# A time budget for VectorE's side work, row scalings on ScalarE, and split fills in neighbouring places, in an attention-with-gradient kernel

## The chip, the cores and the metric

The kernel runs on one core of a Trainium2 chip. The metric is the device time of one execution in microseconds (us). Every kernel was run several times, in alternation with the kernel before on the same chip.

The engines go by short names in the profile. **TensorE** runs matmuls and is called PE in the profile; **VectorE** is DVE, **ScalarE** is ACT, **GpSimd** is POOL, and SP is the engine whose queue issues most DMAs. In this kernel the results of TensorE go to tiles in a memory called **PSUM**, in *banks*; other tiles lie in **SBUF**. A *releaser* is what ended a wait.

## The reference

The reference is a small transformer block with two branches, and the gradient of all its inputs. It was cut here to what matters:

```python
B, T, D, K = (2, 4000, 144, 5)
xa = _layernorm(x)
q, k, v = split(xa @ w_qkv)
p = softmax(q @ k.T * D ** -0.5)
glob = (p @ v) @ w_att_out
h = gelu(xa @ w_mlp_in);  u, g = halves(h);  g = _layernorm(g)
gc = sum(gp[:, i:i + T, :] * dw_csgu[i] for i in range(K))     # 5-tap convolution over time
loc = (u * gc) @ w_mlp_out
m = concat([glob, loc]);  m = m + 5-tap convolution of m
out = x + m @ w_merge
# asked for: out, and the gradients of x and of all seven weights for a given grad_out
```

There are two batches of 4000 rows, which the kernel treats one after the other. Rows come in 32 blocks of 128 (`NBK`), that is 16 *row pairs* (`NPR`).

## The kernel before

For each batch there is one long stage, called *attention* below, in which two kinds of work are interleaved:

- the **global part**: scores, softmax and their gradients, in 129 *units*. A unit is a quarter of one row block; in it TensorE makes four score tiles (`pS` for this unit, `pD` for the one before), ScalarE takes the exponential of `pS`, VectorE makes `Sm = pD * P`. After its unit, TensorE multiplies into `y` and into `X` (the *fills*), whose results are added to `acc` by VectorE (even fills) or by ScalarE and GpSimd (odd fills);
- the **local part** (MLP, layer norm, convolutions), cut into small steps. Each unit has two *places* in which local steps may be issued. For each row pair a Python generator yields before each step: `'V'` for a step without matmuls, `'P'` for one with, and what it must come after.

All of this decides only the order of issue. In the traces an engine works off its list in order (below, ScalarE stands idle for 2.24 us before one instruction while copies stand behind it). The parts that matter:

```python
class Steps:
    def _ready(self, t):
        at, w, _ = t
        if self.now < at: return False
        if w is None: return True
        kind, lag, after = w
        return all(key in self.done and self.now >= self.done[key] + d for key, d in after)
    ...
    def place(self, tensor=True):
        again = True
        while again:                       # every V step that is ready, at once
            again = False
            for t in list(self.tasks):
                if (t[1] is None or t[1][0] == 'V') and self._ready(t):
                    self._step(t)
                    again = True
        if tensor:                         # then one P step
            due = [...]
            if due: self._step(min(due, key=lambda t: t[0]))
        self.now += 1

    def pair(p):                           # local steps of one row pair, cut
        ...
        yield 'V', 2, aft(("dh", 3))       # after the dh of pair p - 3 was issued
        dh = wk.tile([128, 2, 2 * D], BF, tag="dh", bufs=3, name="dh")
        ...
        nc.vector.tensor_tensor(ug[:], h_[:, :, 0:D], gc[:], op=ALU.mult)
        nc.vector.tensor_tensor(du[:], dug[:], gc[:], op=ALU.mult)
        nc.vector.tensor_tensor(dh[:, :, 0:D], du[:], gp[:, :, 0:D], op=ALU.mult)
        ...
        yield 'P', 1, aft(("dg", 1), ("dh", 3), ("wg", 4))
        dgC.put(p, dgc)                    # 4 transposes into PSUM, ScalarE copies out, 16 rows to DRAM
        Q.mark("dg", p)
        yield 'V', 2
        dgC.fill(p)                        # loads the 80 rows of taps that conv needs
        yield 'P', 4, ((("dg", min(p + 1, NPR - 1)), 6),) + aft(("dh", 1))
        pc = dgC.conv(p, True)             # TensorE; waits for the 80-row load
        ...
        nc.vector.tensor_tensor(dh[:, :, D:2 * D], dg[:], gp[:, :, D:2 * D], op=ALU.mult)
        nc.sync.dma_start(S.dh_d[:, 2 * p:2 * p + 2, :], dh[:])
        Q.mark("dh", p)

    def wgrad(p):                          # weight gradient of the convolution
        yield 'V', 2, ((("dg", p), 2),)
        d8 = wk.tile([128, 256], BF, tag="d8", bufs=2, name="d8")
        dgC.taps.spread(d8[0:80, :], p * 256, 256)      # another load from the same DRAM rows
        for m in range(5): ...

    for p in range(NPR):
        Q.add(14 * p, pair(p))
        Q.add(14 * p + 20, wgrad(p))

        def row_end(i):                    # after the last unit of row block i
            nc.vector.reduce_sum(ld[:], ld8[:], axis=AX.X)
            nc.vector.reciprocal(rl[:], ld[:, 0:1])
            nc.vector.tensor_scalar(nd[:], ld[:, 1:2], rl[:], -1.0, op0=ALU.mult, op1=ALU.mult)
            nc.vector.tensor_scalar(Qs[:, pb, :], S.Q_t[:, i, :], rl[:], None, op0=ALU.mult)
            nc.vector.tensor_scalar(br[:], S.B_t[:, i, :], rl[:], None, op0=ALU.mult)
            nc.vector.scalar_tensor_tensor(Bt[:, pb, :], Qs[:, pb, :], nd[:], br[:], op0=ALU.mult, op1=ALU.add)
```

`pm`, `pc`, `ph`, `pj` (local part) and `X` (fills) share three PSUM banks. A fill of a row pair sums over both row blocks of the pair; fills 0 and 1 are split, so that the first block's half can be done early and its bank is held open until the second.

## Time and profile before

| | before |
|---|---|
| median of the first three runs | 1318.11 us (1311.19 to 1318.71) |
| attention, first and second batch | about 66 to 561 us and 696 to 1188 us of the span |
| TensorE busy in attention, by stretch of 33 us | 90 to 99% (the prediction below says 93 to 98%; two stretches with a dip of the clock have 90%) |
| VectorE busy in attention, by stretch of 33 us | 19.9 to 30.4 us |

The first part of the page of the kernel before gives the busy time of each engine, its share of the span and the instructions:

```profile
PE 1222.5 (93%) x15116; PEld 957.1 (73%) x15116; DVE 986.3 (75%) x3421; ACT 806.0 (61%) x2370; POOL 580.4 (44%) x1033
```

TensorE's 93% overstates its work, since records of pipelined matmuls overlap (a 144-column matmul has a record of 226 ns and the next one starts after 62 to 63). I therefore count *gaps* from the starts of the matmuls in the trace. The 144-column matmuls start every 62 to 63 ns when nothing holds them up. Whatever a start comes later than that is a gap, put down to the matmul that came late. It is an estimate, and it comes to 107 us for both batches, of which 6.6 us are what matmuls lost at half clock.

The list of waits of TensorE from 66 to 1196 us, kernel before (what waited, for what: us in total, times, longest us), sees only that part of each gap in which no older matmul was still in its record. It is good for naming the releaser:

```profile
PE X L1925 <- DVE acc L1939: 14.8, 16, 2.8
PE pc L1574 <- DMA gnC<-gnC_d: 9.1, 8, 2.1
PE pD L1854 <- DVE Sm L1868: 7.4, 26, 0.7
PE pm L1545 <- ACT sq L1686: 2.8, 4, 0.8
PE pm L1545 <- ACT dgf L1760: 1.8, 2, 0.9
```

### The profile page before, as it was taken

The numbers are of one execution on the slowest core, as the hardware profiler recorded it, in microseconds if no ns is written. First come the engines' busy times: TensorE is split into PE (matmuls) and PEld (weight loads), VectorE is DVE, ScalarE is ACT, GpSimd is POOL, SyncE is SP. The second block draws the span as 40 slices with busy tenths as digits, with TensorE's granted clock in tenths as the row PEclk, the third lists the DMA queues.
The fourth block names the chain that finished last, engine by engine and source line by source line (L and its number), as shares of the span: only waits on it lengthen the run. The fifth ranks groups of instructions, "written<-read, shape, count | busy, mean of one in ns | idle before, by whom it ended". The sixth has DMA issues, their size and how long they took to land. (4 is left out here: it accounts for less than half of the span.)

```text
span 1318.5 us, 39927 instructions
## 1 busy us (share of the span) xinstructions
PE 1222.5 (93%) x15116; PEld 957.1 (73%) x15116; DVE 986.3 (75%) x3421; ACT 806.0 (61%) x2370; POOL 580.4 (44%) x1033
## 2 busy tenths in 40 slices
PE   4899999999999999999989999999999999999986
PEld 2657776777777777798976677677777777779884
DVE  4666777887989888847735688788798888884664
ACT  2666666667667666546646666666766766654542
POOL 6312445444545454247611244545444544425640
PEclk9999999999999999999999999999999999999999
DMA  6369888887899889987775989888999988998851
GB/s 182 97 126 152 149 153 147 147 149 150 154 164 155 157 141 170 157 190 206 200 218 104 157 145 168 146 146 146 149 152 159 164 151 146 165 159 191 240 151 32
DMA packets 634223, 205.51 MB, mean 156 GB/s; under 512 B 577183, under 2 KB 631556, under 8 KB 633988
## 3 DMA queue, kind: packets, MB, share of 16 engines
q1 hardware_dynamic: 627472, 197.54, 79.3%
q10 hardware_dynamic: 6548, 5.33, 1.8%
q8 instruction: 120, 1.97, 0.6%
q14 instruction: 83, 0.68, 0.2%
HBM read 46.22 MB, written 21.79 MB: 52 GB/s over the span
## 5 line engine op out<-in xcount | busy, mean ns | idle before, releaser
L1868 DVE SCALAR_TENSOR_TENSOR Sm<-pD,Pm 128x500 bf16<-128x500 f32 x512 | 325.6, 673 | 104.0 <-PE pD L1858 71.4
L1866 ACT ACTIVATE Pm<-pS 128x500 bf16<-128x500 f32 x512 | 295.4, 584 | 99.6 <-PE pS L1858 96.8
L1925 PE MATMUL X<-Qs,Sm 128*128 128x144 bf16 x2048 | 286.5, 226 | 15.3 <-DVE acc L1939 14.8
L1937 POOL TENSOR_TENSOR acc<-xs,acc 128x432 f32<-128x432 f32 x150 | 172.3, 1148 | 268.3 <-ACT xs L1936 267.9
L1926 PE MATMUL X<-Bt,Pm 128*128 128x144 bf16 x2048 | 286.4, 226 | 0.8 <-DVE Bt L1890 0.8
L1926 PEld LDWEIGHTS <-Pm 128*128 128x128 bf16 x2048 | 200.6, 98 | 19.4 <-issue 18.4
L1925 PEld LDWEIGHTS <-Sm 128*128 128x128 bf16 x2048 | 200.5, 98 | 2.2 <-issue 1.0
L1903 PEld LDWEIGHTS <-ST 128*128 128x128 bf16 x2048 | 137.8, 98 | 28.2 <-issue 1.1
L1903 PEld LDWEIGHTS <-PT 128*128 128x128 bf16 x2048 | 137.4, 98 | 28.3 <-issue 0.5
L1936 ACT COPY xs<-X 128x432 f32<-128x432 f32 x150 | 77.7, 518 | 127.4 <-PE X L1926 113.9
L1939 DVE TENSOR_TENSOR acc<-X,acc 128x432 f32<-128x432 f32 x180 | 104.0, 578 | 65.6 <-PE X L1926 65.2
L1854 PE MATMUL pD<-rb,QBr 16*128 16x500 bf16 x448 | 100.8, 379 | 7.3 <-DVE Sm L1868 6.6
L1866 ACT ACTIVATION_READ_ACCUMULATOR Pm<-pS 128x1 f32 x512 | 103.3, 202 | 0.0
L1854 PE MATMUL pS<-rb,QBr 16*128 16x500 bf16 x448 | 92.4, 382 | 2.5 <-ACT Pm L1866 2.4
L1858 PEld LDWEIGHTS <-BTm 128*128 128x128 bf16 x512 | 50.0, 98 | 59.3 <-issue 1.5
L1785 DVE SCALAR_TENSOR_TENSOR jg<-gnC,dgC 128x256 bf16<-128x256 bf16 x160 | 92.0, 575 | 1.3
L1858 PEld LDWEIGHTS <-QTm 128*128 128x128 bf16 x512 | 29.1, 97 | 75.8 <-issue 75.8
L1913 POOL TENSOR_TENSOR B_t<-zd,yd 128x144 bf16<-128x144 f32 x64 | 34.3, 537 | 111.5 <-ACT zd L1912 111.5
L1892 POOL TENSOR_SCALAR nr<-nd,rl 128x1 f32<-128x1 f32 x64 | 20.5, 320 | 136.9 <-DVE nd L1886 136.7
L1858 PE MATMUL pS<-rb,QTm 128*128 128x500 bf16 x256 | 77.3, 384 | 0.0
L1858 PE MATMUL pS<-ra,QTm 128*128 128x500 bf16 x256 | 76.9, 382 | 0.0
L1858 PE MATMUL pD<-rb,BTm 128*128 128x500 bf16 x256 | 75.7, 377 | 0.0
(626 smaller groups left out, 2949.6 us busy)
## 6 DMA issues: line engine op xcount, KB each, us to landing
gs<-in_grad_out_dram SPq DMA_DIRECT2D x24, 720.0 KB
dh_d<-dh SPq DMA_DIRECT2D x32, 144.0 KB
dhr<-dh_d SPq DMA_DIRECT2D x16, 288.0 KB
gs<-in_grad_out_dram SPq DMA_DIRECT2D x8, 540.0 KB
xg<-in_x_dram SPq DMA_DIRECT2D x21, 144.0 KB
dug_d<-dug SPq DMA_DIRECT2D x16, 144.0 KB
dug<-dug_d SPq DMA_DIRECT2D x32, 72.0 KB
ug_d<-ug SPq DMA_DIRECT2D x32, 72.0 KB
```

The costliest lines, as they stand in the source:

```text
L1785: nc.vector.scalar_tensor_tensor(jg[:], a_[:, m:m + 256], 1.0, d_[:, 2:258], op0=ALU.mult, op1=ALU.mult, accum_out=dws[:, p, m:m + 1])
L1854: nc.tensor.matmul(o_[h][:, 0:SC], jt[i // 4][2][rr, i % 4, :], S.XR[c2][rr, 0:SC], start=True, stop=False)
L1858: nc.tensor.matmul(o_[h][:, 0:SC], jt[i // 4][w][:, i % 4, :], S.xaT[:, c0:c0 + SC], start=False, stop=True)
L1866: nc.scalar.activation(P[:, pb, c1:c1 + SC], o_[h][:, 0:SC], ACT.Exp, accum_out=ld8[:, 0, n_:n_ + 1])
L1868: nc.vector.scalar_tensor_tensor(Sm[:, pb, c1:c1 + SC], o_[h][:, 0:SC], 1.0, P[:, pb, c1:c1 + SC], op0=ALU.mult, op1=ALU.mult, accum_out=l ...
L1903: nc.tensor.matmul(y[:, w, :], src[:, jj, :], S.xaa[:, j, :], start=(j == 0), stop=(j == NBK - 1))
L1913: nc.gpsimd.tensor_tensor(S.Zn[:, i, :], zd[:], yd[:], op=ALU.add)
L1925: nc.tensor.matmul(X[:, jj, :], Sm[:, i % NP, j * 128:(j + 1) * 128], Qs[:, i % 4, :], start=(kk == 0 and jj == 0), stop=False, skip_group ...
L1926: nc.tensor.matmul(X[:, jj, :], P[:, i % NP, j * 128:(j + 1) * 128], Bt[:, i % 4, :], start=False, stop=(kk == 1), skip_group_check=True)
L1936: nc.scalar.copy(xs[:, 0:nj, :], X[:, 0:nj, :])
L1937: nc.gpsimd.tensor_tensor(a_, xs[:, 0:nj, :], a_, op=ALU.add)
L1939: nc.vector.tensor_tensor(a_, X[:, 0:nj, :], a_, op=ALU.add)
```

## The change

The intent: VectorE is busy 75% of the time and yet late, since its local steps come in lumps. So (1) a budget lets only so much VectorE time be issued per place; with it come a sorting of the tasks by the time they were set for, and a slightly closer start of the row pairs; (2) two row scalings move to ScalarE, which has time; (3) the two halves of a split fill move into neighbouring places, so that two of the three PSUM banks are held for a shorter time.

```diff
 class Steps:
+    def __init__(self, rate, most):
+        self.left, self.rate, self.most = most, rate, most
+    def use(self, cost):
+        self.left -= cost
     def _ready(self, t):
-        return all(key in self.done and self.now >= self.done[key] + d for key, d in after)
+        return all(key in self.done and self.now >= self.done[key] + d for key, d in w[2]) and (w[3] == 0 or w[0] != 'V' or self.left >= w[3] / 2)
     def _step(self, t):
+        if t[1]:
+            self.left -= t[1][3]
     def place(self, tensor=True):
+        self.left = min(self.left + self.rate, self.most)
-            for t in list(self.tasks):
+            for t in sorted(self.tasks, key=lambda t: t[0]):
 ...
-        yield 'V', 2, aft(("dh", 3))
+        yield 'V', 2, aft(("dh", 3)), 1.1          # each V step now names its cost in us
 ...                                               # (one step is split in two)
-        Q.add(14 * p, pair(p))
-        Q.add(14 * p + 20, wgrad(p))
+        Q.add(27 * p // 2, pair(p))
+        Q.add(27 * p // 2 + 20, wgrad(p))
 ...
-            nc.vector.tensor_scalar(Qs[:, pb, :], S.Q_t[:, i, :], rl[:], None, op0=ALU.mult)
+            nc.scalar.activation(Qs[:, pb, :], S.Q_t[:, i, :], ACT.Copy, scale=rl[:])
-            nc.vector.tensor_scalar(br[:], S.B_t[:, i, :], rl[:], None, op0=ALU.mult)
+            nc.scalar.activation(br[:], S.B_t[:, i, :], ACT.Copy, scale=rl[:])
+            Q.use(1)
 ...
-        fills = {(1, 0): ..., (7, 1): ((0, (0,)), (1, (0,)))}
+        fills = {(0, 1): ((0, (0,)), (1, (0,))), (1, 0): ...}      # the rest as before
-        Q = Steps()
+        Q = Steps(1.15, 1.4)
 ...                                               # the adds of the fills call Q.use(.6)
+                if i == NBK:                      # after the last row block
+                    Q.rate = Q.most = 1.8
```

More of the change, by code (lines that the diff above doesn't have):

```diff
@@ L1599 @@
 class Steps:
-    def __init__(self):
+    def __init__(self, rate, most):
         self.now, self.done, self.tasks = 0, {}, []
+        self.left, self.rate, self.most = most, rate, most
     def add(self, at, gen):
@@ L1618, in _ready @@
             return True
-        kind, lag, after = w
-        return all(key in self.done and self.now >= self.done[key] + d for key, d in after)
+        return all(key in self.done and self.now >= self.done[key] + d for key, d in w[2]) and (w[3] == 0 or w[0] != 'V' or self.left >= w[3] / 2)
     def _step(self, t):
+        if t[1]:
+            self.left -= t[1][3]
         try:
@@ L1627, in _step @@
             return
-        w = (w + ((),))[:3] if len(w) < 3 else w
+        w = tuple(w) + ((), 0)[len(w) - 2:]
         t[0], t[1] = self.now + w[1], w
     def place(self, tensor=True):
+        self.left = min(self.left + self.rate, self.most)
         again = True
@@ L1692, in pair @@
         nc.gpsimd.tensor_scalar(t3[:], sq[:], 6 * K0 * K1, 2 * K0, op0=ALU.mult, op1=ALU.add)
-        yield 'V', 2
+        yield 'V', 2, (), .5
         nc.vector.tensor_tensor(a_[:], a_[:], hs[:], op=ALU.mult)
@@ L1697, in pair @@
         nc.scalar.activation(a_[:], a_[:], ACT.Tanh)
-        yield 'V', 2, aft(("ug", 4))
+        yield 'V', 2, aft(("ug", 4)), .8
         h_ = wk.tile([128, 2, 2 * D], BF, tag="h_t", bufs=4, name="h_t")
@@ L1702, in pair @@
         Q.mark("h", p)
-        yield 'V', 1
+        yield 'V', 1, (), .95
         mv = sm.tile([128, 2, 2], F32, tag="mvg", name="mv")
@@ L1716, in pair @@
         nc.gpsimd.tensor_tensor(oq[:], oq[:], h_[:], op=ALU.mult)
-        yield 'V', 2, aft(("dh", 6))
+        yield 'V', 2, aft(("dh", 6)), 1.2
         nm = sm.tile([128, 2], F32, tag="nmg", name="nm")
@@ L1738, in pair @@
         nc.scalar.copy(gc[:], pc[:])
+        yield 'V', 0, (), .45
         dgc = wk.tile([128, 2, D], BF, tag="dgc", bufs=2, name="dgc")
         nc.vector.tensor_tensor(dgc[:], dug[:], h_[:, :, 0:D], op=ALU.mult)
-        yield 'V', 2, aft(("dh", 3))
+        yield 'V', 2, aft(("dh", 3)), 1.1
         dh = wk.tile([128, 2, 2 * D], BF, tag="dh", bufs=3, name="dh")
@@ L1760, in pair @@
             nc.scalar.activation(dg[:, q, :], pc[:, q, :], ACT.Copy, scale=rs[:, q:q + 1], accum_out=s12[:, 0, q:q + 1])
-        yield 'V', 2
+        yield 'V', 2, (), 1.1
         jk = jg[:, 0:D]
@@ L1770, in pair @@
             nc.gpsimd.tensor_scalar(cc[:, q, :], gn[:, q, :], n12[:, 1, q:q + 1], n12[:, 0, q:q + 1], op0=ALU.mult, op1=ALU.add)
-        yield 'V', 2
+        yield 'V', 2, (), .75
         nc.vector.tensor_tensor(dg[:], dg[:], cc[:], op=ALU.add)
@@ L1783, in wgrad @@
         for m in range(5):
-            yield 'V', 1
+            yield 'V', 1, (), .6
             nc.vector.scalar_tensor_tensor(jg[:], a_[:, m:m + 256], 1.0, d_[:, 2:258], op0=ALU.mult, op1=ALU.mult, accum_out=dws[:, p, m:m + 1])
-        yield 'V', 1
+        yield 'V', 1, (), .6
         nc.vector.scalar_tensor_tensor(jg[0:80, :], gnC.kept8.pop(p)[0:80, :], 1.0, d8[0:80, :], op0=ALU.mult, op1=ALU.mult, accum_out=dw8[0:80, p:p + 1])
@@ L1933, in xfill @@
                 (nc.scalar.copy if f % 2 else nc.vector.tensor_copy)(a_, X[:, 0:nj, :])
+                Q.use(0 if f % 2 else .6)
             elif f % 2 == 1:
@@ L1938, in xfill @@
             else:
+                Q.use(.6)
                 nc.vector.tensor_tensor(a_, X[:, 0:nj, :], a_, op=ALU.add)
-        fills = {(1, 0): ((0, (1,)), (1, (1,))), (1, 1): ((2, (0, 1)),), (2, 1): ((3, (0, 1)),), (3, 0): ((4, (0, 1)),), (3, 1): ((5, (0, 1)),),
-                 (4, 1): ((6, (0, 1)),), (5, 0): ((7, (0, 1)),), (5, 1): ((8, (0, 1)),), (6, 0): ((9, (0, 1)),), (6, 1): ((10, (0, 1)),), (7, 1): ((0, (0,)), (1, (0,)))}
-        Q = Steps()
+        fills = {(0, 1): ((0, (0,)), (1, (0,))), (1, 0): ((0, (1,)), (1, (1,))), (1, 1): ((2, (0, 1)),), (2, 1): ((3, (0, 1)),), (3, 0): ((4, (0, 1)),), (3, 1): ((5, (0, 1)),),
+                 (4, 1): ((6, (0, 1)),), (5, 0): ((7, (0, 1)),), (5, 1): ((8, (0, 1)),), (6, 0): ((9, (0, 1)),), (6, 1): ((10, (0, 1)),)}
+        Q = Steps(1.15, 1.4)
         local_steps(k, W, b, S, es, ps_f, Q)
@@ L1962, in phase_attn @@
                         for f, rows in fills.get((half * 4 + c2, place), ()):
-                            q = pr + 1 if rows == (0,) else pr
-                            if 0 <= q < NBK // 2:
-                                xfill(q, f, rows)
+                            if 0 <= pr < NBK // 2:
+                                xfill(pr, f, rows)
                         Q.place()
```

## The prediction

> **What bounds it now.** Each of the two batches spends about 495 us (66-561 and 696-1188 us of the span) in the attention stage; the change touches only that. There the windows view shows TensorE busy 93-98%, but busy times overlap. The timeline shows 144-column matmuls starting every 62-63 ns[...]. Counting starts that way (the four 16-row matmuls of a unit run together in about 0.32 us), I estimate 436 us of real work and 51-54 us of gaps per batch. TensorE is the bound, at about 89%; only the gaps, about 105 of 1318 us, can be won.
>
> By the instruction that came late, both batches: pD (waits for VectorE to finish Sm) 28 us; X (waits for a PSUM bank that VectorE's acc add frees) 19; pS 28, of which about 26 is a fixed 0.1 us per unit; the convolution pc (waits for its 80-row DMA) 10; transposes pm 6. So about 50 us hang on a late VectorE, though it is busy only 24-30 of 33 us per window: it is late in lumps. From issue order and measured durations, VectorE's work between Sm pairs averages 3.30 us, standard deviation 1.02; 36 of 127 intervals exceed the 3.9 us pace, up to 5.8.
>
> **What the change does.**
> 1. The budget evens VectorE's work. Same count in the changed order: standard deviation 0.74, maximum 4.8, 17 over, excess 23 -> 7 us per batch. Here is the gain.
> 2. Qs and br go to ScalarE: VectorE loses 254 + 288 ns for each of 64 rows, 35 of its 986 us. ScalarE gains two one-pointer ACTIVATEs per row: [...]the trace has 0.38 for the like zd and yd. About +50 us on ScalarE (806 -> 855), not the bound. But Bt stays next in VectorE's order after nd, so VectorE now waits about 0.5 us for ScalarE: less busy, Bt hardly earlier. ScalarE waits for rl. Worth nothing or slightly negative.
> 3. Split fills keep two of three PSUM banks open for two places instead of four; 12 matmuls now stand before the second row's Bt is needed, covering the longer row end. A few us fewer X and pm waits.
>
> Matmuls, DMA and the other stages stay; put-to-convolution distance stays three units, so pc's wait stays.
>
> **Time.** Estimate: 60% of pD and X waits (28 us), 3 of pm, minus about 6 of new ScalarE-VectorE waits: -25 us. **Predicted 1293 us, 80% range 1278-1309.** Faster by over 2%: 0.44; within 2%: 0.53; slower: 0.03.
>
> **What would show it.** Attention about 12 us shorter per batch, the rest unchanged. TensorE waits pD<-Sm and X<-acc less than half. VectorE busy about 950, with new idle before Bt, released by ScalarE's br, 0.3-0.6 us x 64. ScalarE about 855, idle before Qs released by VectorE's rl. The pc wait on DMA still about 10 us.
>
> **What would make it wrong.** ScalarE, held behind Qs, delays exps, so pS and then Sm wait. DMA engines, 79-100% busy here, may fall behind a faster TensorE, so flips or 80-row loads arrive late. Or gaps merely move to another releaser. On the other side, fewer gaps could also remove the three clock dips in attention (3.4-6.8 us at half clock), and the gain exceeds 30 us.

28 us of pD and X waits and 3 of pm, less 6 for new waits, are the 25 us that lead from 1318 to 1293. The +50 us on ScalarE, which are not in the sum, follow from 0.38 us in the trace for each of 128 instructions.

## More of the kernel before

The fills wait for a bank that VectorE frees, the score tiles for VectorE's `Sm`, the forward convolution for the load of its taps. The backward convolution's load (`dgC<-dgC_d`) does not appear.

The timeline of the SP queue, kernel before, shows why (start us, us, engine, line, operation, out<-in). The load of the taps, L1527, is issued ahead of the spread, L1524, and ahead of two transposing DMAs that occupy the queue for 2 to 3 us each:

```profile
370.93 0.40 SPq L1520 DMA_DIRECT2D dgC_d<-dgC0s  x1
371.37 0.43 SPq L1663 DMA_DIRECT2D Rz<-R_d  x1
373.30 0.31 SPq L1527 DMA_DIRECT2D dgC<-dgC_d  x1
373.66 0.75 SPq L1524 DMA_DIRECT2D d<-dgC_d  x1
374.52 2.81 SPq L1876 DMA_TRANSPOSE ST<-Sm  x1
377.42 2.38 SPq L1876 DMA_TRANSPOSE PT<-Pm  x1
```

Two stretches from the windows view, kernel before (stretch, length, busy us of each engine with its count, then granted clock, DMA share, GB/s), for comparison later:

```profile
66.00:312.00 246.00, 233.59 (x2693) 172.23 (x2693) 184.67 (x620) 159.82 (x478) 97.73 (x161) 0.98 0.84 147
529.00:560.00 31.00, 29.50 (x358) 22.02 (x355) 27.06 (x96) 17.33 (x56) 8.82 (x18) 1.00 0.95 165
```

## The result, and the profile after

The changed kernel was slower: 1331.85 us (median of four runs, 1330.61 to 1333.88) against 1316.66 us (four runs, 1311.19 to 1318.71), a ratio of 1.0123 with a 95% interval of 1.0089 to 1.0158. Ratios here and below are the mean time of one kernel's fast runs over that of the kernel before in the same rounds, so not quite the ratio of the medians that are quoted.

The first part of the page, kernel after:

```profile
PE 1226.7 (92%) x15116; PEld 959.4 (72%) x15116; DVE 962.1 (72%) x3293; ACT 843.2 (63%) x2498; POOL 561.5 (42%) x1033
```

VectorE lost 24 us of busy time (35 predicted) and ScalarE gained 37 us (about 50 predicted). The waits of TensorE from 66 to 1196 us, kernel after:

```profile
PE pc L1574 <- DMA dgC<-dgC_d: 16.6, 11, 2.8
PE X L1933 <- DVE acc L1949: 15.4, 12, 4.4
PE pm L1545 <- ACT dgC L1549: 6.3, 2, 3.2
PE pD L1861 <- DVE Sm L1875: 4.0, 18, 0.5
PE pc L1574 <- DMA gnC<-gnC_d: 1.6, 3, 0.7
```

Three lines are new or changed. The backward convolution now waits 16.6 us for its load; the longest wait for a bank grew from 2.8 to 4.4 us; the transposes `pm` wait twice for 3.2 us. Three lines of the waits of ScalarE and VectorE in the same stretch, kernel after, have no counterpart before:

```profile
ACT Qs L1894 <- DVE rl L1891: 71.0, 59, 4.1
...
DVE Bt L1898 <- ACT br L1896: 33.9, 63, 0.5
...
DVE dh L1754 <- DMA dh_d<-dh: 6.0, 2, 3.7
```

The windows view, kernel after, for the same two stretches:

```profile
66.00:312.00 246.00, 235.70 (x2757) 173.73 (x2756) 188.78 (x608) 175.01 (x529) 99.14 (x171) 0.99 0.88 153
529.00:560.00 31.00, 26.26 (x301) 19.28 (x299) 21.45 (x76) 16.10 (x51) 8.45 (x17) 0.94 0.91 157
```

In the first stretch TensorE did 2757 matmuls where it had done 2693. In the second it did 301 where it had done 358. So the changed kernel is *ahead* for half of the stage and then loses it. Units 8 to 56 of the first batch took 181.6 us (before 188.9); units 120 to 128 took 36.2 us (before 30.6), and in the second batch 35.4 us (30.6).

TensorE's gaps from the trace, by the instruction that was late, both batches. *Cold* is what matmuls lost by running at half clock; *all* contains it and some smaller ones:

| us | pD | pS | X | pc | pm | cold | all |
|---|---|---|---|---|---|---|---|
| before | 28.6 | 28.4 | 20.5 | 13.4 | 5.8 | 6.6 | 107 |
| after | 23.0 | 26.4 | 24.0 | 22.9 | 6.9 | 12.8 | 119 |

The largest gaps fall at the same units in both batches, so they belong to the order of issue. Three chains explain them.

**The dh store (unit 122).** The chain that ended last, kernel after (start us, us, what):

```profile
536.32 0.31 DVE dh L1780
536.62 0.03 DVE ug L1752
536.65 3.97 DMA dh_d<-dh
...
540.94 1.28 DVE Sm L1875 x4
542.22 0.53 DVE acc L1949
542.75 0.04 issue
542.79 0.28 PE X L1933
```

The last write of an old pair's `dh` (L1780) and the first write of a new pair's `dh` (L1754, after L1752 and L1753) now come together. With three buffers the new write must wait until the store of the old one, issued a moment before, has landed. VectorE stands for 3.65 us of it, and a gap of 4.56 us on TensorE follows. The condition in the code, `("dh", 3)`, asks only that the step of the old pair has been *issued*; it says nothing of the store.

**The row scalings (unit 65).** ScalarE's timeline, kernel after:

```profile
307.72 0.21 ACT L1873 ACTIVATION_READ_ACCUMULATOR Pm<-pS 128x1 f32 x1
310.17 0.41 ACT L1894 ACTIVATE Qs<-Q_t,rl 128x144 bf16<-128x144 bf16 x1 [2.24 <-DVE rl L1891]
310.49 0.40 ACT L1896 ACTIVATE br<-B_t,rl 128x144 f32<-128x144 bf16 x1
310.91 0.36 ACT L1548 COPY dgC0s<-pm 32x256 bf16<-32x256 bf16 x1
311.30 0.37 ACT L1549 COPY dgC<-pm 128x256 bf16<-128x256 bf16 x1
```

ScalarE stands idle 2.24 us before `Qs`, until VectorE has `rl`. Behind `Qs` in its list are the copies that empty a PSUM bank (`dgC<-pm`). The next transposes `pm` need it and start at 311.73, after a gap of 3.33 us.

**The load behind the spread.** The SP queue, kernel after, where the same place of the before kernel was shown above:

```profile
370.30 0.40 SPq L1520 DMA_DIRECT2D dgC_d<-dgC0s  x1
370.79 3.01 SPq L1883 DMA_TRANSPOSE ST<-Sm  x1
373.89 1.97 SPq L1883 DMA_TRANSPOSE PT<-Pm  x1
375.96 0.94 SPq L1524 DMA_DIRECT2D d<-dgC_d  x1
376.95 0.45 SPq L1527 DMA_DIRECT2D dgC<-dgC_d  x1
```

The spread (L1524) has gone ahead of the load (L1527), and here both come after the two transposing DMAs. In the traces the two are issued one right after the other 30 times; before, the load was first in all 30, after, the spread was. The cause is the sorting. The weight-gradient task's time was set long ago, so it sorts ahead of the pair's task, although nobody waits for its load soon. The budget can hardly have done it: neither of the two steps has a cost. The other traces agree: of the kernels without the mend below, the spread is first all 30 times in those that sort (after, e1_vec, e2_dh4, e5_after, e10_budget_only), and the load all 30 times in those that don't (before, e6_act_only, e7_fill_only, e13_spacing_only).

These were readings. The experiments had to show what each chain costs.

### The profile page after: what moved, and what is told of

The parts are those of the page before. It is cut to its first block, busy times and chain, and to the rows that moved or that the text cites. A ratio compares the mean times of both kernels' runs of the same rounds, so it can differ in the third digit from the quotient of the medians.

```text
span 1328.8 us, 39888 instructions
## 1 busy us (share of the span) xinstructions
PE 1226.7 (92%) x15116; PEld 959.4 (72%) x15116; DVE 962.1 (72%) x3293; ACT 843.2 (63%) x2498; POOL 561.5 (42%) x1033
## 4 chain that ended last, share of the span: by engine, by line
PE 65%; DVE 12%; DMA 10%; issue 4%; ACT 4%; POOL 2%; SPq 2%; ACTq 0%; DVEq 0%; POOLq 0%
PE y L1911 14%; PE pS L1865 8%; PE X L1933 8%; PE X L1934 7%; PE pD L1865 6%; PE pS L1861 5%; DVE Sm L1875 4%; PE pc L1573 2%; PE pb L1467 2%; DMA dgC<-dgC_d 2%; PE po L2088 1%; PE EF L2063 1%; PE gr L2159 1%; DMA u<-r 1%; DVE acc L1949 1%
## 5 line engine op out<-in xcount | busy, mean ns | idle before, releaser
L1933 PE MATMUL X<-Qs,Sm 128*128 128x144 bf16 x2048 | 286.4, 227 | 18.4 <-DVE acc L1949 15.4
L1946 POOL TENSOR_TENSOR acc<-xs,acc 128x432 f32<-128x432 f32 x150 | 167.5, 1117 | 297.9 <-ACT xs L1945 297.1
L1861 PE MATMUL pD<-rb,QBr 16*128 16x500 bf16 x448 | 97.7, 381 | 3.7 <-DVE Sm L1875 3.2
L1792 DVE SCALAR_TENSOR_TENSOR jg<-gnC,dgC 128x256 bf16<-128x256 bf16 x160 | 88.5, 553 | 1.0
L1911 PE MATMUL y<-ra,PT 128*128 128x144 bf16 x1024 | 76.2, 229 | 0.0
L1865 PE MATMUL pD<-ra,BTm 128*128 128x500 bf16 x256 | 76.2, 379 | 0.0
```

The lines of the kernel that those rows point to most:

```text
L1792: nc.vector.scalar_tensor_tensor(jg[:], a_[:, m:m + 256], 1.0, d_[:, 2:258], op0=ALU.mult, op1=ALU.mult, accum_out=dws[:, p, m:m + 1])
L1861: nc.tensor.matmul(o_[h][:, 0:SC], jt[i // 4][2][rr, i % 4, :], S.XR[c2][rr, 0:SC], start=True, stop=False)
L1865: nc.tensor.matmul(o_[h][:, 0:SC], jt[i // 4][w][:, i % 4, :], S.xaT[:, c0:c0 + SC], start=False, stop=True)
L1911: nc.tensor.matmul(y[:, w, :], src[:, jj, :], S.xaa[:, j, :], start=(j == 0), stop=(j == NBK - 1))
L1933: nc.tensor.matmul(X[:, jj, :], Sm[:, i % NP, j * 128:(j + 1) * 128], Qs[:, i % 4, :], start=(kk == 0 and jj == 0), stop=False, skip_group ...
L1946: nc.gpsimd.tensor_tensor(a_, xs[:, 0:nj, :], a_, op=ALU.add)
```

## The experiments

All kernels gave correct results. Each was run six times or so (five rounds and the profiled run). The last column is the ratio to the kernel before in the same rounds. e1 to e4, e5 to e8, e9 to e12 and e13 to e16 were each one call of runs on one chip; between calls only ratios are compared, and that is less certain. In the column *mends*, dh and spread are the two edits explained below.

| | rows on | fills | pacing | mends | median us | before us | ratio (95%) |
|---|---|---|---|---|---|---|---|
| after (first result) | ScalarE | new | yes | none | 1331.85 | 1316.66 | 1.0123 (1.0089–1.0158) |
| e1_vec | VectorE | new | yes | none | 1326.64 | 1321.47 | 1.0039 (1.0014–1.0064) |
| e2_dh4 | ScalarE | new | yes | dh | 1328.08 | 1321.47 | 1.0053 (1.0028–1.0077) |
| e3_spread | ScalarE | new | yes | spread | 1328.00 | 1321.47 | 1.0048 (1.0017–1.0079) |
| **e4_all3** | VectorE | new | yes | dh, spread | **1303.36** | 1321.47 | **0.9869** (0.9846–0.9892) |
| e5_after | ScalarE | new | yes | none | 1334.69 | 1318.29 | 1.0129 (1.0091–1.0166) |
| e6_act_only | ScalarE | old | no | none | 1327.36 | 1318.29 | 1.0085 (1.0048–1.0121) |
| e7_fill_only | VectorE | new | no | none | 1312.58 | 1318.29 | 0.9968 (0.9934–1.0003) |
| e8_old_fill | VectorE | old | yes | dh, spread | 1308.17 | 1318.29 | 0.9940 (0.9904–0.9977) |
| e9_rows_in_mended | ScalarE | new | yes | dh, spread | 1316.53 | 1315.89 | 1.0008 (0.9979–1.0038) |
| e10_budget_only | VectorE | old | yes | none | 1334.21 | 1315.89 | 1.0144 (1.0111–1.0176) |
| e11_no_pacing | VectorE | new | no, rest of bundle | dh, spread | 1329.82 | 1315.89 | 1.0118 (1.0096–1.0140) |
| e12_later_conv | VectorE | new | yes | dh, spread, conv | 1307.20 | 1315.89 | 0.9955 (0.9925–0.9985) |
| e13_spacing_only | VectorE | old | spacing only | none | 1325.25 | 1314.76 | 1.0085 (1.0054–1.0117) |
| e14_old_spacing | VectorE | new | yes, 14 places | dh, spread | 1303.01 | 1314.76 | 0.9911 (0.9885–0.9936) |
| e15_no_sort | VectorE | new | yes, no sort | dh, spread | 1303.78 | 1314.76 | 0.9905 (0.9877–0.9933) |
| e16_no_bundle | VectorE | new | none of bundle | dh, spread | 1313.74 | 1314.76 | 0.9988 (0.9958–1.0018) |

### One mend at a time

**e1_vec**: the scalings back on VectorE, all other order as in the changed kernel.

```diff
-            nc.scalar.activation(Qs[:, pb, :], S.Q_t[:, i, :], ACT.Copy, scale=rl[:])
-            nc.scalar.activation(br[:], S.B_t[:, i, :], ACT.Copy, scale=rl[:])
+            nc.vector.tensor_scalar(Qs[:, pb, :], S.Q_t[:, i, :], rl[:], None, op0=ALU.mult)
+            nc.vector.tensor_scalar(br[:], S.B_t[:, i, :], rl[:], None, op0=ALU.mult)
```

> The changed kernel with the two row scalings (Qs, br) back on VectorE; budget, order of all other instructions and fills as changed. Theory A (the new cross-engine waits cost: ScalarE is held in order behind Qs until VectorE has rl, as at unit 65, where the transposes wait 3.3 us for a PSUM bank that ScalarE should have emptied): the two 3.3 us gaps before the gn transposes go, with the clock dip after the first; 6 to 10 us faster than the changed kernel, about 1323. Rival B (the row scalings are neutral or help, the loss is elsewhere): within 3 us of the changed kernel or slower, because VectorE gets 35 us of work back.

Measured: 1.0039 where the changed kernel has 1.0123 and 1.0129, so about 0.9% or 11 us less. The two 3.3 us gaps at unit 65 are gone from the trace; units 64 to 72 of the first batch take 29.9 us, where the changed kernel's two profiles have 35.0 and 32.3. Theory A holds, the gain a little above what I had expected. (The profiled run was the slowest of the six, 1333.78 us, so sums of its waits are not used.)

**e2_dh4**: four `dh` buffers. The 1.1 KB per partition come from the `dgC8` buffers, of which two are free long before.

```diff
-        dh = wk.tile([128, 2, 2 * D], BF, tag="dh", bufs=3, name="dh")
+        dh = wk.tile([128, 2, 2 * D], BF, tag="dh", bufs=4, name="dh")
-   ... tag=self.name + "8", bufs=4, ...
+   ... tag=self.name + "8", bufs=4 if self.name[0] == "g" else 2, ...
```

> The changed kernel with four dh buffers in place of three (room for it from two of the four dgC8 buffers, which are long free); same order on every engine. Theory A (at unit 122 of each batch VectorE waits 3.7 us for the store of dh to land, because the budget puts the last write of pair p-3's dh and the first write of pair p's dh into one place): the X gaps of 4.6 and 3.7 us there and their clock dips go, units 120 to 128 take about 31 us instead of 36.2 and 35.4; 8 to 10 us faster, about 1322. Rival B (the units there are slow because the work of local steps piles up at the end, whatever the buffer): the same 35 to 36 us, no gain.

Measured: 1.0053, about 0.7% or 10 us less. Units 120 to 128 take 31.6 and 31.0 us, and VectorE's wait for the store is gone from its list. The order on each engine is the same, so it was the wait and not the amount of work. What the two fewer `dgC8` buffers cost, if anything, was not tested apart: TensorE waits 21.0 us for the `dgC` load here (16.6 and 17.4 in the changed kernel's two profiles). One line of TensorE's waits, e2_dh4, which in the changed kernel has 15.4 in total and 4.4 for the longest:

```profile
PE X L1933 <- DVE acc L1949: 8.7, 11, 1.2
```

**e3_spread**: the spread one place later, the compute order the same.

```diff
-        dgC.taps.spread(d8[0:80, :], p * 256, 256)
         for m in range(5):
             yield 'V', 1, (), .6
+            if m == 0:
+                dgC.taps.spread(d8[0:80, :], p * 256, 256)
```

> The changed kernel with the spread load of the weight gradient issued one place later, so that the 80-row load of dgC stands first in the DMA queue again, as before the change; compute order the same. Theory A (sorting the tasks by their time put the spread, which is not urgent, ahead of the load that the convolution waits for): TensorE's wait of pc on the dgC load falls from 16.6 us to under 6; 8 to 12 us faster, about 1321. Rival B (the store is what is late, or the DMA engines are full, and the order of two loads does not matter): the wait stays above 13 us and the time within 3 us.

Measured: 1.0048, about 0.8% or 10 us less. TensorE's waits for the two loads, e3_spread, against 16.6 and 1.6 in the changed kernel:

```profile
PE pc L1574 <- DMA gnC<-gnC_d: 6.7, 10, 1.1
...
PE pc L1574 <- DMA dgC<-dgC_d: 5.7, 9, 1.7
```

The order of two small loads in the queue decided it, and not the transposing DMAs: at the place shown before they still stand ahead of the load (370.10 and 373.05), SP queue, e3_spread:

```profile
369.59 0.41 SPq L1520 DMA_DIRECT2D dgC_d<-dgC0s  x1
...
375.30 0.74 SPq L1527 DMA_DIRECT2D dgC<-dgC_d  x1
376.10 0.75 SPq L1524 DMA_DIRECT2D d<-dgC_d  x1
```

With the spread behind the load, the wait fell from 16.6 us to 5.7. No run separates the spread's place in the queue from the time that its issue takes in the SP queue (0.94 us above, by which the load is issued sooner here). A part of it moved to the forward convolution's load, 1.6 to 6.7.

**e4_all3**: the three edits together.

> All three of these edits together in the changed kernel. Theory A (three accidents of the new order took back what the evener VectorE had won): the gains add, 20 to 28 us faster than the changed kernel, 1303 to 1311, which is 5 to 12 us faster than the kernel before. Rival B (the gaps move to another releaser when one is closed): less than 12 us gained, still slower than the kernel before.

Measured: 1303.36 us against 1321.47, ratio 0.9869. That is 2.5% less than the changed kernel; one by one the three had given 0.9, 0.7 and 0.8%. So the gains add, to a little more than expected, and the mended kernel beats both kernels. TensorE's waits, e4_all3:

```profile
PE pc L1574 <- DMA dgC<-dgC_d: 9.1, 9, 2.6
PE X L1934 <- DVE acc L1950: 8.8, 11, 1.4
PE pc L1574 <- DMA gnC<-gnC_d: 5.5, 8, 1.8
PE pD L1862 <- DVE Sm L1876: 4.3, 18, 0.5
```

The gaps sum to 92 us here (107 before, 119 after), the cold part to 3.1 us (6.6 and 12.8). The cold part is worth a remark. The trace lists when the granted clock was halved, in attention always for 3.4 us or twice that. There were three such dips before, six after, and two here. Each of the six began within 5 us of the start of one of the large gaps (1.95 to 4.56 us); the second batch's gap of 3.33 us at unit 65 had none. So in the changed kernel six of the seven gaps of 1.95 us and more in attention were followed by such a dip, and so paid for again. In its trace the dips have a clock of 0.5, and the starts of the six lie whole multiples of 3.413 us apart (20, 48, 88, 50 and 47 of them).

### The three parts by themselves

**e5_after** is the changed kernel once more, beside the parts.

> The changed kernel as it is, once more, on the same chip as the single parts below, to have its loss beside them. Expected: 1.012 times the kernel before, within 0.003.

Measured: 1.0129. The loss is repeatable.

**e6_act_only**: the kernel before with the edit of e1_vec reversed.

> The kernel before with only the two row scalings on ScalarE; order of all else the same. Theory A (ScalarE held in order behind Qs until VectorE has rl costs on its own, wherever VectorE is late): 3 to 12 us slower than the kernel before, and ScalarE waits for rl over 50 us in total. Rival B (it hurts only together with the budget's order, where one place put all of a unit's work ahead of the row end): within 3 us.

Measured: 1.0085, about 11 us slower by itself; theory A. ScalarE waits 72.2 us for `rl` in all. What got worse is not the exponentials: `pS` waits 2.7 us (2.4 before). The transposes `pm` got worse, which wait for a bank behind ScalarE's copies. TensorE's waits, e6_act_only, against 2.8 and 1.8 before:

```profile
PE pm L1545 <- ACT sq L1686: 4.7, 4, 1.7
PE pm L1545 <- ACT dgf L1760: 4.3, 2, 2.2
```

By the gap count `pm` rose from 5.8 to 10.1 us, which is less than half of the loss; the rest is spread over small changes that I did not resolve.

**e7_fill_only**: the kernel before with the new `fills` table and its use.

> The kernel before with only the new place of the split fills; nothing else moves. My prediction's theory (banks are held for two places instead of four, so fewer waits for a bank): 2 to 5 us faster. Rival (the empty place only moves from the first to the last unit of a row pair, and the second rows' fill, with twelve more matmuls ahead of it, comes later): within 2 us or slower.

Measured: 0.9968, with an interval that just touches 1; 4 us faster by the ratio. It is as I had predicted for this part, but not certain from this run alone. By the gap count X fell from 20.5 to 14.0 us and `pm` from 5.8 to 1.9.

**e8_old_fill**: e4_all3 with the old `fills` table.

> The kernel before with the budget alone, and the two order accidents mended (four dh buffers, the spread one place later): that is the mended kernel of the experiment before (rows on VectorE) with the old place of the split fills. If the evener VectorE is what pays: 9 to 17 us faster than the kernel before, 0.987 to 0.993. If the new fills pay for most of the gain of the mended kernel: within 5 us of the kernel before.

Measured: 0.9940, just above the range of the first theory. The budget with the mends gives 0.6%; the new fills add about 0.7% to it in this order (0.9869 in another call of runs).

**e9_rows_in_mended**: e4_all3 with the scalings on ScalarE.

> The mended kernel (budget, new fills, four dh buffers, the spread one place later) with the two row scalings on ScalarE again; order as in the changed kernel. If the three costs are separate and add: 10 to 14 us slower than the mended kernel with rows on VectorE, so 0.995 to 1.000 of the kernel before, with the 3.3 us gap before the gn transposes at unit 65 back in both batches. If the rows cost only beside the other accidents: within 4 us of it (0.987 to 0.990).

Measured: 1.0008, so the scalings cost 1.4% or 18 us in the mended order, more than alone. The `pm` wait at unit 65 is back with exactly its old size; of e9_rows_in_mended:

```profile
PE pm L1545 <- ACT dgC L1549: 6.3, 2, 3.2
```

**e10_budget_only**: the kernel before with the budget's bundle (pacing, sorting, spacing), nothing else. 

> The kernel before with the budget alone (sorted tasks, costs, spacing 13.5), rows on VectorE, old fills, nothing mended. From the experiments so far: the mended one is 0.994, and the dh store and the spread cost about 9 and 10 us: 1.003 to 1.011. If it is below 1.000, the two accidents do not belong to the budget's order but to its meeting with the other two parts.

Measured: 1.0144, worse than expected. The two accidents are all there without the other parts: TensorE waits 19.2 us for the `dgC` load, and before the fill at unit 122 there are gaps of 4.13 and 3.66 us in the two batches. With the mends the same is 0.9940 (e8_old_fill), so dh store and spread together cost about 2%.

### What in the bundle pays

**e11_no_pacing**: e4_all3 with a budget that never holds anything back.

```diff
-        Q = Steps(1.15, 1.4)
+        Q = Steps(99, 99)
-                    Q.rate = Q.most = 1.8
+                    Q.rate = Q.most = 99
```

> The mended kernel with the budget made so large that it never holds a step back; sorted tasks, spacing 13.5, new fills and the mends stay. VectorE's work between Sm pairs then has a standard deviation of 1.08 us (0.82 in the mended kernel, 1.02 before). Theory A (evening VectorE's work is what pays): 6 to 15 us slower than the mended kernel, 0.991 to 0.999. Rival B (the gain of the mended kernel comes from the fills, the earlier start of the pairs and the mended waits, not from evening): within 4 us of it, 0.985 to 0.990.

Measured: 1.0118, 2.5% slower than the mended kernel, and so far outside both expectations. Its first half is fast all the same (units 8 to 56 in 181.7 and 179.2 us), and it loses later, with waits for both convolution loads (13.4 and 8.0 us) and seven clock dips. So this run alone did not show that evening pays. The bundle had to be taken apart further.

**e12_later_conv**: e4_all3 with the backward convolution two places later (`8` for `6` after the next pair's `dg`).

> The mended kernel with the backward convolution two places later after the next pair's dgC transposes (8 for 6), to see whether what is left of its DMA wait (9.1 us in the mended kernel, up to 2.6 us at unit 80) can be had. If the wait is a matter of lead time: wait under 3 us and 3 to 8 us faster than the mended kernel, about 0.982. If the later chain pushes the local steps together at the end: no gain or slower.

Measured: 0.9955, no gain. The wait for the `dgC` load is gone from the list, but the forward convolution's load now waits 20.8 us in all. The wait moved from one load to the other.

**e13_spacing_only**: the kernel before with pairs every 13.5 places.

```diff
-        Q.add(14 * p, pair(p))
-        Q.add(14 * p + 20, wgrad(p))
+        Q.add(27 * p // 2, pair(p))
+        Q.add(27 * p // 2 + 20, wgrad(p))
```

> The kernel before with only the closer start of the pairs (13.5 places for 14). VectorE's work gets lumpier (standard deviation 1.11 us, 28 us over the pace per batch, before 1.02 and 23). Theory S (closer spacing makes the early gain of all changed kernels, units 8 to 56 in 181 us for 189): it takes about 182 us there, and the whole is 0.990 to 0.998. Theory P (pacing makes it): 188 us or more there and no gain in total, or a loss.

Measured: 1.0085. The closer spacing by itself costs 0.85%. Units 8 to 56 took 184.0 and 187.0 us in the two batches, between the two theories; what was won was lost later, with 19.6 us of waits for the `gnC` load (9.1 before).

**e14_old_spacing**: e4_all3 with 14 places.

> The mended kernel with the old start of the pairs (14 places). Work between Sm pairs 0.85 us standard deviation (mended 0.82). Theory S: the early gain goes (units 8 to 56 in 186 us or more) and the time is 0.993 to 1.000 of the kernel before. Theory P: within 0.4% of the mended kernel, 0.984 to 0.991.

Measured: 0.9911, theory P by its speed in units 8 to 56 (179.9 and 179.6 us) and just at the edge by its total. With pacing, the early gain does not need the closer spacing.

**e15_no_sort**: e4_all3 with `list(self.tasks)` for `sorted(...)`.

> The mended kernel without the sorting of tasks by time. If the sorting does nothing but put the spread ahead of the load (which the mend takes back): within 0.4% of the mended kernel, 0.984 to 0.991. If the sorting carries a good part of the gain: 0.993 or more.

Measured: 0.9905, within the 0.4% of e4_all3 that was set as the mark. The two were not run in the same call, and whether the sorting is worth the 0.36% between them is not decided: the intervals overlap. Without the sorting the harmful exchange of the two loads would not have come about: no kernel that doesn't sort shows it.

**e16_no_bundle**: no pacing, no sorting, 14 places; the new fills and the mends stay.

> The mended kernel with neither pacing, nor sorting, nor closer spacing: what is left of the change is the new fills, four dh buffers, the later spread and the split of one step in two. If the pacing is needed for the mended gain: like the fills alone, 0.994 to 1.000. If the mends or the fills carry it: 0.984 to 0.991.

Measured: 0.9988, like the kernel before (units 8 to 56: 189 us; before 188.9). So the mends are worth nothing where the bundle has not made them necessary, and pacing with sorting is worth 0.8% (e14_old_spacing against e16_no_bundle, same rounds and spacing). Pacing without sorting (e15_no_sort) stands just as well, at 0.9905, though with the closer spacing. The gap count says where: pD is 25.6 us without the bundle, 27.9 in e11_no_pacing, and 21.4, 21.7 and 13.6 in the paced e4_all3, e14_old_spacing and e15_no_sort.

## Why the prediction was wrong

The prediction was 1293 us, faster by 1.9%, with 1309 as its upper end. Measured was a loss of 1.2%. The step that failed is the sum under "Time". It credits evener VectorE work with 28 us of waits won and charges the new order with 6. The runs show about 10 us for pacing, and against it about 30: 11 for the scalings on ScalarE, 10 for the store of dh and 10 for the load behind the spread. Point by point:

- **"TensorE is the bound ... only the gaps can be won": right.** The matmul work stayed; the difference of the two kernels is in the gaps and in the dips of the clock that follow on gaps (the cold part 6.6 to 12.8 us; 107 to 119 us in all by the count, where the two profiled spans differ by 10.3).
- **"Here is the gain" (evening VectorE): right in kind, wrong in size.** I took 28 us, as "60% of pD and X waits". In the changed kernel pD fell from 28.6 to 23.0 us, a fifth, and X rose from 20.5 to 24.0. Shown by e14_old_spacing against e16_no_bundle, pacing (with the sorting) is worth 0.8%, about 10 us. Part of the error was my count of VectorE's lumps: moving `Qs` and `br` out took them out of the count (standard deviation 0.74 us), but VectorE waits for their results in the same spot, 33.9 us in all. Counted in the same order with the scalings on VectorE, it is 0.82 us, with 14.9 us of excess for each batch instead of 7.2. (Checked on the traces with each operation's median duration, first batch: excess 27.6 us before, 8.7 after, 17.4 in e1_vec.)
- **"Worth nothing or slightly negative" (scalings on ScalarE): the sign right, the size wrong.** I allowed 6 us for all new waits between ScalarE and VectorE. The scalings alone cost about 11 us (e1_vec, e6_act_only) and 18 us in the mended order (e9_rows_in_mended). The cost of the instructions was nearly right: `Qs` took 414 and `br` 399 ns, against 0.38 us for the like `zd` and `yd` in the trace before, and VectorE's idle before `Bt` was 0.54 us each time (33.9 us / 63), as predicted. What I had not asked is what stands *behind* them in ScalarE's list. I had named late exponentials as the danger; what the traces show late is the copies that empty PSUM banks (in e6_act_only they explain less than half of the loss; the rest stays open).
- **"put-to-convolution distance stays three units, so pc's wait stays": this step failed outright.** The distance stayed, but the wait went from 9.1 us (for `gnC`, before) to 18.2 us (16.6 for `dgC`, 1.6 for `gnC`). The lead time counts from the issue of the load, and its place in the DMA queue had changed. e3_spread shows it: 10 us.
- **Not in the prediction at all: the wait of VectorE on the store of dh**, about 10 us (e2_dh4). The prediction spoke of a buffer only for PSUM. It looked at how much work each unit had, not at which buffers that work needed.
- **"A few us fewer X and pm waits" (fills): right**, 4 us alone (e7_fill_only), about 0.7% in the mended order.

In short, the sum was +10 us for pacing and up to 9 for the fills, less 11 for the scalings and about 10 each for the two accidents, with the clock dips contained in each. These are estimates from different pairs of kernels, and they do not close to the microsecond: pacing and spacing act on each other, as e11_no_pacing and e13_spacing_only show (the closer spacing costs 11 us alone and is not in the sum). What remains open is how much of pacing's value comes from evening VectorE and how much from shifting in time the loads that the convolutions wait for; with another order, both change.

## What to carry to other kernels

When a scheduler is changed, count not only how evenly it spreads an engine's work. Look through the new order for pairs that have come together: a store and the next write of its buffer, a load that someone waits for and one that nobody waits for, a wait for another engine and the PSUM evictions behind it. Moving instructions to an engine that was idle 39% of the time, ScalarE, was not free here, since the input was not always ready when their turn came: the copies behind `Qs` inherited its wait of 2.24 us, and TensorE got a gap of 3.33 us. Where a change that should help does not, look for the stretch in which it is ahead: here half of the stage showed that the idea was sound and that three separate waits, each with a mend of a few lines, had eaten it.

## What else the traces show

- Gaps before the clock dips: in the kernel before, the three dips in attention began within 4 us of the start of gaps of about 2.3, 2.9 and 2.9 us. In the changed kernel two of the six followed gaps of 2.95 us and 2.51 us, each within 4 us, while the gap of 3.33 us at unit 65 of its second batch had no dip. So their length alone does not tell them apart.
- The store of `dh`: 144 KB took 3.97 us from its issue until VectorE was released (4.29 in e3_spread), beside a transposing DMA and with the DMA engines 91% busy (window 529 to 560 us).
- An ACTIVATE of 144 columns with one pointer operand: 0.41 us (`Qs`) and 0.40 us (`br`) in the changed kernel. Ahead of PSUM evictions, 2.24 us of waiting for `rl` became a gap of 3.33 us on TensorE.
